# A fused attention + state-space gradient kernel: part of GpSimd's table work moved from the attention loop to the channel loop, and matmul bursts placed in other half-steps

## The chip, the cores and the metric

The kernel runs on one core of one Trainium2 chip. The metric is the device time of one execution in microseconds (us); lower is better. Before the change three runs gave 3099.37, 3094.06 and 3100.29 us, median 3099.37.

## What is computed

The reference is a forward pass and its gradients. For one sequence of S = 2048 tokens of width D = 576 it mixes two branches with a sigmoid gate and returns the output and twelve gradients for a given `grad_out` (bfloat16 in and out):

```
qkv = x @ wqkv;  a = softmax(q k^T / sqrt(18)) v @ wo            # 32 heads of width 18
P[d,n,l] = exp(dt[d] * A[d,n] * l),  l = 0..2047, N = 128 states  # complex
K[d,l]   = Re sum_n C[d,n] dt[d] B[d,n] P[d,n,l]
b = causal_convolution(u, K) + u * Dskip
out = g * a + (1 - g) * b,   g = sigmoid(sum(x * gate_w))
outputs: out, and d/d(x, wqkv, wo, A, B, C (re and im), log_dt, Dskip, gate_w)
```

What matters here: the convolution works in blocks of 128 positions and needs, for each channel d and state n, the table E[d] of complex powers z^l with z = exp(dt A), l = 0..127. It depends on the parameters alone, so it can be made at any time before its channel is worked on.

## The kernel before

**Stages.** One stage after the other: projections and parameters (to about 206 us of the profiled span), attention forward and backward (206 to 2302), the channel loop of the state-space branch (2302 to 2874), and the final products.

**Attention** (line 339 on) goes by units: 8 groups of 4 heads x 4 blocks of 512 queries = 32 units. A unit has 32 half-steps, and G counts them over all units. In half-step G TensorE makes two row-tiled matmuls of the forward pass (`P1`: tile ps_P<-QaT_g,KaT_g, line 709), and, for the unit that lies OFF = 39 half-steps behind, two matmuls of recomputed scores (`P3`: ps_P<-KaT_g,QaT_g) and two of the probability gradient (`P2`: ps_P<-dOaT,VaT_g). ScalarE makes exp of P1 (tile PT, line 802) and exp of P3 (tile eb, line 807); VectorE multiplies P2 by PT (tile ds, line 812, two a half-step). P1 and P3 share two PSUM buffers (tag S), P2 has two of its own (dP).

Besides, each half-step has one burst, by its phase `ph` = (G - 39) % 4, into one PSUM buffer (tag accB) that VectorE then empties:

| ph | burst | filler matmuls ahead of it (NFILL) | emptied by VectorE |
|---|---|---|---|
| 0 | accV, 8 matmuls | 0 | dvacc, line 508 |
| 1 | accQ, 8 matmuls | 0 | dqa, line 528 |
| 2 | accK, 16 matmuls | 1 | dkacc, line 556 |
| 3 | dst_p, 4 transposes of ds; in one half-step of a unit instead the transposes of the forward result (accF, line 411) | 3 | dsT, line 464; or rl, Ob |

A filler multiplies one constant by another (J_bf by ident_bf, tile accF or accK) and its result is overwritten. The forward sum accO<-PT,Vtok_g (4 matmuls for every second half-step's worth of PT, line 741) is issued in the half-steps of phase 0 and 1, after P2. The order on TensorE is by hand: P1(G), burst of G - 1, P3(G), P2(G), accO if it is due. At the end of a unit's forward pass the accO sum is copied (oT, line 407), transposed (f1), divided by its row sums (rl, Ob, lines 416 and 419), GpSimd makes dOa and prod (lines 421 and 423), and VectorE's dl (line 429) needs prod (f2).

**GpSimd in attention.** It makes all of E: 36 groups of CE = 16 channels, each of 78 instructions. 30 of them are small (powers of z, tiles eT and eG); then come 8 pairs of channels of 6 instructions each (two products et<-eG,eT and one sum Eo<-et,et, 128x256, for the real and again for the imaginary part, line 571), and after every second pair a DMA writes 4 channels to DRAM (E_d<-Eo, line 619). The instructions stand in a list with estimated costs; `e_emit(G)` issues the share due at half-step G, between G = 10 and 994, and nothing in the first three half-steps of a unit. GpSimd also packs gradients (dtk, line 446, and the DMA dqkv_d, line 447) and issues the DMAs put_x and put_gy (lines 663 and 667).

**Channel loop** (line 1136): 18 blocks of 32 channels, iteration i = -1 to 17. VectorE runs the scan of block i: 14 dependent steps of three instructions (tz line 997, tz line 1000, HG line 1001), then wa and wb (1016), Rw (1022, 1023), and the products pq (1067, 1095). ScalarE casts hR and gR (1008) between scan and pq, and in every second iteration prepares RX (891 to 893) ahead of these. TensorE turns E (etp, 958), and makes uvp, yp and the sums of pq. E comes back from DRAM in halves of a block (1 MB each, tile E1n, line 967, six buffers). GpSimd only makes two small sums an iteration, SS<-m, lines 1103 and 1104. The order on the compute engines is that of the code; DMA issues on SP are placed by the scheduler.

Of the kernel before, what the change touches and what calls it, by code (L numbers as in the profile page):

```python
# [20 lines left out]
def build(tc, aps, dbg_aps=None, stages=("s1", "attn", "post", "s4", "final")):  # L21
# [40 lines left out]
    with ExitStack() as gctx:  # L62
# [274 lines left out]
        go_v = go2.rearrange("(t p) d -> p t d", p=P)  # L337
        x_v = x2.rearrange("(t p) d -> p t d", p=P)
        if "attn" in stages:
            KB = 512  # L340
            NQ = S // KB
            TPQ = KB // P
            DA = HP
            NFILL = (0, 0, 1, 3)
            with ExitStack() as ctx:
# [212 lines left out]

                CE = 16
                EH = 4  # L560
                NA, NBT = P // 16, 16
                T_ = work.tile([P, 2, CE, NBT + 1], F32, tag="eT", bufs=1, name="eT")
                G_ = work.tile([P, 2, CE, NA], F32, tag="eG", bufs=1, name="eG")
                for t_ in (T_, G_):
                    nc.gpsimd.memset(t_[:, 0, :, 0], 1.0)
                    nc.gpsimd.memset(t_[:, 1, :, 0], 0.0)
                eops = []
                ez = {}

                def pl(out, a, b, op):  # L570
                    nc.gpsimd.tensor_tensor(out, a, b, op=op)  # L571

                def e_tmp(k):
                    return work.tile([P, 2 * P], F32, tag=f"et{k}", bufs=1, name=f"et{k}")

                def load_z(k):
                    ez[k] = work.tile([P, 2, CE], F32, tag="ez", bufs=2, name="ez")
                    nc.gpsimd.dma_start(ez[k], par_d[:, 12:14, k * CE:(k + 1) * CE])

                def emit_power(dst, src, lo, n, sq):  # L580

                    x = src[:, :, :, 1:1 + n]
                    st = []

                    def mul(ri):
                        w_ = e_tmp(ri)[:, 0:2 * CE * n].rearrange("p (r c m) -> p r c m", r=2, c=CE)
                        pl(w_, x, sq[:, ri].unsqueeze(1).unsqueeze(3).to_broadcast([P, 2, CE, n]), A.mult)
                        st.append(w_)
                    est = 0.21 + 2 * CE * n * 0.0018
                    eops.append((est, lambda: mul(0)))  # L590
                    eops.append((est, lambda: mul(1)))
                    est = 0.2 + CE * n * 0.002
                    eops.append((est, lambda: pl(dst[:, 0, :, lo:lo + n], st[0][:, 0], st[1][:, 1], A.subtract)))
                    eops.append((est, lambda: pl(dst[:, 1, :, lo:lo + n], st[0][:, 1], st[1][:, 0], A.add)))

                Eo = {}

                def e_main(k, c):
                    q = k * CE + c
                    for ri in range(2):  # L600
                        st = []

                        def mul(gi, ti, st):
                            if ti == gi == 0 and q % EH == 0:
                                Eo[q // EH] = work.tile([P, EH, 2, P], BF, tag="Eo", bufs=2, name="Eo")
                            w_ = e_tmp(gi)
                            pl(w_.rearrange("p (c a b) -> p c a b", c=2, b=NBT),
                               G_[:, gi, c:c + 2, :].unsqueeze(3).to_broadcast([P, 2, NA, NBT]),
                               T_[:, ti, c:c + 2, 0:NBT].unsqueeze(2).to_broadcast([P, 2, NA, NBT]), A.mult)
                            st.append(w_.rearrange("p (c l) -> p c l", c=2))  # L610

                        def add(ri, st):
                            o_ = Eo[q // EH][:, q % EH:q % EH + 2, ri, :]
                            if ri == 0:
                                pl(o_, st[1], st[0], A.subtract)
                            else:
                                pl(o_, st[0], st[1], A.add)
                                if (q + 2) % EH == 0:
                                    nc.gpsimd.dma_start(E_d[:, q + 2 - EH:q + 2], Eo.pop(q // EH))
                        eops.append((0.64, lambda mul=mul, ri=ri, st=st: mul(0, ri, st)))  # L620
                        eops.append((0.64, lambda mul=mul, ri=ri, st=st: mul(1, 1 - ri, st)))
                        eops.append((0.74 + 1.0 * (ri == 1 and (q + 2) % EH == 0), lambda add=add, ri=ri, st=st: add(ri, st)))

                for k in range(D // CE):
                    eops.append((0.25, lambda k=k: nc.gpsimd.tensor_copy(T_[:, :, :, 1], ez.pop(k))))
                    for n in (1, 2, 4, 8):
                        emit_power(T_, T_, n + 1, n, T_[:, :, :, n])
                    eops.append((0.25, lambda: nc.gpsimd.tensor_copy(G_[:, :, :, 1], T_[:, :, :, NBT])))
                    for n, m in ((1, 1), (2, 2), (4, 3)):
                        emit_power(G_, G_, n + 1, m, G_[:, :, :, n])  # L630
                    if k + 2 < D // CE:
                        eops.append((0.0, lambda k=k: load_z(k + 2)))
                    for c in range(0, CE, 2):
                        e_main(k, c)
                e_total = sum(x[0] for x in eops)
# [17 lines left out]
                for g0, nm, g, m in sorted(lds):  # L653
                    if g0 < 0:
                        load_piece(nm, g, m)
                    else:
                        at(("pre", g0), lambda nm=nm, g=g, m=m: load_piece(nm, g, m))
                for k in range(2):
                    at(("pre", 4), lambda k=k: load_z(k))
                NTOT = NU * NST  # L660
# [22 lines left out]
                for G in range(NTOT + OFF + 24):  # L683
# [48 lines left out]
                    tail = []  # L732
                    if G % 4 in (3, 0) and G >= 3:
                        i_ = (G - 3) // 4 * 2 + (1 if G % 4 == 0 else 0)
                        u_, i_ = divmod(i_, NT)
                        if u_ < NU:
                            g, b = units[u_]
                            if i_ == 0:
                                accO[(g, b)] = apsp.tile([P, KB], F32, tag="accO", name="accO")
                            for j in range(4):  # L740
                                mm(accO[(g, b)][HP * j:HP * (j + 1), :], lhsT=grp_t[g]["Vtok", i_ // TPQ][:, i_ % TPQ, HS * j:HS * j + HP], rhs=UN[(g, b)]["PT"][i_][:, j, :],
                                   start=(i_ == 0), stop=(i_ == NT - 1), tile_position=(0, HP * j))
                            if i_ == NT - 1:
                                f0, f1, f2 = post_forward(g, b, accO.pop((g, b)))
                                tail.append(f0)
                                at(("f1", G + 2), f1)
                                at(("f2", G + 4), f2)

                    def late(G=G, G2=G2, ph=ph):

                        evs = []
                        if ph in (0, 1, 2):
                            ACC.append(accB(("accV", "accQ", "accK")[ph]))
                            fill(ACC[0], NFILL[ph])
                        elif 0 <= G2 < NTOT or ("f1", G) in todo:
                            acc_f = accB("accF")
                            fill(acc_f, NFILL[3])
                            for f in todo.pop(("f1", G), []):
                                evs.append(f(acc_f))
# [68 lines left out]
                assert not todo and not packs, (todo.keys(), packs)  # L828
                assert e_done[1] == len(eops) and not Eo
        if "s4" in stages:  # L830
# [11 lines left out]
            with ExitStack() as ctx:  # L842
# [122 lines left out]
                def load_en(b, h):  # L965
                    dG = b * CB + h * GS
                    En = blk(b)["En"][h] = pw.tile([P, GS, 2, P], BF, tag="E1n", bufs=6, name="E1n")
                    nc.sync.dma_start(En, E_d[:, dG:dG + GS])
# [137 lines left out]
                def t0_load(b):  # L1106
# [5 lines left out]
                    nc.sync.dma_start(T0w.rearrange("p j c -> p (j c)"), src)  # L1112

                m_load(0)
                load_rx(0)
# [16 lines left out]
                load_en(2, 0)  # L1132
                load_en(2, 1)
                m_part(1, 0)
                m_part(1, 1)
                for i in range(-1, NBLK):
# [28 lines left out]
                    if cur:  # L1165
                        if nx:
                            t0_load(i + 1)
                        ybp(i, 0)
                        ybp(i, 1)
                        pairs1(i)  # L1170
                    if cur and mb is not None:
                        load_en(mb, 0)
                        load_en(mb, 1)
                    if sb is not None:
                        turn_e(sb, 0, 0, 4)
                        m_sum(sb)
                        m_fin(sb)
                    if cur:
                        pairs2(i)
# [262 lines left out]
```

## Time and profile before

| what | value |
|---|---|
| median of three runs | 3099.37 us |
| the profiled execution's own time | 3094.2 us |
| its span, first to last instruction | 3092.5 us |
| busy: PE, DVE, ACT, POOL | 2608.6, 2464.7, 2395.3, 1799.7 us |
| mean granted TensorE clock | 0.921 |
| HBM read and written | 144.48 MB, 99.69 MB |

PE is TensorE's matmul (PEld its weight load), DVE VectorE, ACT ScalarE, POOL GpSimd, SP the engine that issues most DMAs. A group of instructions is named by line, engine, operation and out<-in tiles; "idle before" is the time for which its engine stood still just ahead of it. A DMA's line is that of its issue. Most TensorE instructions are recorded by a helper on line 30 and are told apart by tile.

### The profile page before, as it was taken

The page shows a single profiled execution, that of the slowest core. Times are in us where ns is not written, and L with a number is a line of the kernel's source. Part 1 is how long each engine was busy: PE and PEld are TensorE (multiplying, and loading weights), DVE is VectorE, ACT ScalarE, POOL GpSimd, SP SyncE. Part 2 cuts the span into 40 slices and gives each one's busy share as a digit, 9 for nine tenths or more (in the row PEclk, how much of TensorE's full clock was granted, in tenths as well). Part 3 has the DMA queues.
Part 4 walks back from the last instruction along what each step waited for, and adds up shares of the span by engine and source line. Part 5 has one row for each costly group of instructions (what it writes and reads, how often), then busy time and mean ns, then how long its engine had stood idle before and what let it go on. Part 6 is the DMA issues. An engine that isn't in the chain of part 4 may idle for free. (4 is left out here: it accounts for less than half of the span.)

```text
span 3092.5 us, 70491 instructions
## 1 busy us (share of the span) xinstructions
PE 2608.6 (84%) x27147; PEld 1202.5 (39%) x27147; DVE 2464.7 (80%) x4531; ACT 2395.3 (77%) x2765; POOL 1799.7 (58%) x3371
## 2 busy tenths in 40 slices
PE   4768999899899899889889989989866887786679
PEld 2432232232233233223223323323225777776347
DVE  4436898898899899889889989989964888888634
ACT  2458999999899899999899989989836677675111
POOL 0038888988888889888898888988110000000010
PEclk8878999999999899999999999999987888888789
DMA  8757999899989999989998998898788887772885
GB/s 221 154 142 129 173 165 180 156 168 166 163 166 164 170 163 165 178 158 167 164 165 163 172 171 159 167 172 162 133 151 243 213 208 204 206 200 79 228 205 132
DMA packets 1409063, 529.41 MB, mean 171 GB/s; under 512 B 1303487, under 2 KB 1378849, under 8 KB 1399509
## 3 DMA queue, kind: packets, MB, share of 16 engines
q1 hardware_dynamic: 1380212, 464.27, 78.5%
q0 software_dynamic: 20624, 53.26, 6.6%
q10 hardware_dynamic: 7888, 7.38, 0.8%
q8 instruction: 212, 3.47, 0.4%
q14 instruction: 127, 1.03, 0.1%
HBM read 144.48 MB, written 99.69 MB: 79 GB/s over the span
## 5 line engine op out<-in xcount | busy, mean ns | idle before, releaser
L812 DVE TENSOR_TENSOR ds<-ps_P,PT 128x512 bf16<-128x512 f32 x2048 | 1312.3, 681 | 18.5 <-PE ps_P L30 14.4
L807 ACT ACTIVATE eb<-ps_P 128x1024 bf16<-128x1024 f32 x1024 | 1058.1, 1033 | 125.1 <-PE ps_P L30 120.7
L802 ACT ACTIVATE PT<-ps_P 128x1024 bf16<-128x1024 f32 x1024 | 1058.7, 1037 | 41.1 <-PE ps_P L30 39.1
L571 POOL TENSOR_TENSOR et<-eG,eT 128x256 f32<-128x256 f32 x1152 | 700.1, 629 | 35.5
L30 PE MATMUL ps_P<-dOaT,VaT_g 32*128 32x512 bf16 x2048 | 561.9, 390 | 51.3 <-DVE ds L812 43.8
L30 PE MATMUL ps_P<-QaT_g,KaT_g 32*128 32x512 bf16 x2048 | 413.6, 398 | 124.7 <-ACT PT L802 110.0
L571 POOL TENSOR_TENSOR Eo<-et,et 128x256 bf16<-128x256 f32 x576 | 418.7, 727 | 42.4
L30 PE MATMUL ps_P<-KaT_g,QaT_g 32*128 32x512 bf16 x2048 | 406.2, 389 | 1.4 <-ACT eb L807 1.0
L1103 POOL TENSOR_TENSOR SS<-m 128x96 f32<-128x96 f32 x18 | 7.8, 431 | 556.9 <-ACT m L1101 556.9
L30 PEld LDWEIGHTS <-KaT_g 32*128 32x128 bf16 x2048 | 135.4, 92 | 432.7 <-issue 430.9
L30 PEld LDWEIGHTS <-QaT_g 32*128 32x128 bf16 x2048 | 114.9, 91 | 310.4 <-issue 288.3
L30 PE MATMUL accF<-ident_bf,J_bf 128*128 128x512 bf16 x783 | 225.8, 399 | 10.0 <-DVE gb L556 10.0
L30 PE MATMUL accO<-PT,Vtok_g 128*32 128x512 bf16 x2048 | 213.2, 403 | 0.0
L464 DVE COPY dsT<-dst_p 128x512 bf16<-128x512 bf16 x224 | 95.0, 424 | 111.0 <-PE dst_p L463 109.9
L30 PEld LDWEIGHTS <-J_bf 128*128 128x128 bf16 x1103 | 89.1, 100 | 226.3 <-issue 194.6
L30 PE MATMUL accK<-dsT,Qtok_g 128*32 128x256 bf16 x4096 | 166.0, 284 | 0.0
L30 PE MATMUL accQ<-ds,Ktok_g 128*32 128x512 bf16 x2048 | 158.9, 387 | 2.8 <-DVE gb L508 1.5
L30 PE MATMUL accV<-eb,dOa 128*32 128x512 bf16 x2048 | 159.0, 388 | 2.2 <-DVE dsT L464 1.6
L959 ACT COPY E1e<-etp 128x1024 bf16<-128x1024 bf16 x144 | 135.8, 1040 | 16.8 <-PE etp L958 16.8
L30 PE MATMUL yp<-Rw,E1n 128*128 128x30 bf16 x1152 | 67.7, 232 | 83.7 <-DVE Rw L1022 69.1
L30 PEld LDWEIGHTS <-E1n 128*128 128x128 bf16 x2304 | 96.7, 109 | 101.2 <-issue 100.7
L508 DVE TENSOR_TENSOR dvacc<-dvacc,accV 128x512 f32<-128x512 f32 x192 | 130.1, 678 | 0.1
(243 smaller groups left out, 3911.6 us busy)
## 6 DMA issues: line engine op xcount, KB each, us to landing
E_d<-Eo POOLq DMA_DIRECT2D x144, 256.0 KB, 3.9
E1n<-E_d SPq DMA_DIRECT2D x36, 1024.0 KB
xs<-xb_d SPq DMA_DIRECT2D x18, 1024.0 KB
T0w<-Kp_d SPq DMA_DIRECT2D x18, 1024.0 KB
Md_d<-mst SPq DMA_DIRECT2D x36, 288.0 KB
dsT<-ds SPq DMA_TRANSPOSE x512
dqkv_d<-dtk POOLq DMA_DIRECT2D x96, 72.0 KB, 4.4
QKV_d<-stg SPq DMA_DIRECT2D x12, 504.0 KB
```

The lines of the kernel that those rows point to most:

```text
L30: return nc.tensor.matmul(out, lhsT=lhsT, rhs=rhs, start=start, stop=stop, **kw)
L464: return lambda: nc.vector.tensor_copy(U["dsT", p][:, 1, 0:TPQ, :], pt_)
L508: nc.vector.tensor_tensor(o_, a_, acc, op=A.add)
L571: nc.gpsimd.tensor_tensor(out, a, b, op=op)
L802: nc.scalar.activation(U["PT"][i][:, j:j + 2, :], ps, ACT.Exp)
L807: nc.scalar.activation(e, ps, ACT.Exp)
L812: nc.vector.tensor_tensor(U["ds"][i][:, j, :], ps, U["PT"][i][:, j, :], op=A.mult)
L959: nc.scalar.copy(E_[:, 4 * q:4 * q + 4], pt_)
L1103: nc.gpsimd.tensor_tensor(o_[:, :, 0], m4[:, :, 0], m4[:, :, 3], op=A.subtract)
```

## The change

1. The last four of the 18 channel blocks, that is the last 8 of 36 groups of E, are no longer made in attention. The code of the list becomes a function `basis_ops(pool, k0, k1)`, used for groups 0 to 27 in attention and for groups 28 to 35 in the channel loop. There `basis_share(i)` issues a fifteenth of the 624 instructions in each of the iterations -1 to 13, ahead of `pairs2` and `sums` of that iteration.
2. Forward sums move from phases 0 and 1 to phases 3 and 2 (`G % 4` 3, 0 becomes 2, 1); f1 follows the last one at one half-step instead of two, f2 at three instead of four.
3. Fillers: NFILL goes from (0, 0, 1, 3) to (1, 0, 0, 2), and to none where f1's transposes come.
4. E1n has five buffers instead of six, and the second half of block i + 2 is loaded in iteration i between the two ybp, not with its first half one iteration earlier.

```diff
-            NFILL = (0, 0, 1, 3)
+            NFILL = (1, 0, 0, 2)
...
-                for k in range(D // CE):
+            for k in range(k0, k1):
...
+                eops, load_z01 = basis_ops(work, 0, KE)
...
-                    if G % 4 in (3, 0) and G >= 3:
-                        i_ = (G - 3) // 4 * 2 + (1 if G % 4 == 0 else 0)
+                    if G % 4 in (2, 1) and G >= 2:
+                        i_ = G // 4 * 2 - (1 if G % 4 == 1 else 0)
...
-                                at(("f1", G + 2), f1)
-                                at(("f2", G + 4), f2)
+                                at(("f1", G + 1), f1)
+                                at(("f2", G + 3), f2)
...
-                            fill(acc_f, NFILL[3])
+                            fill(acc_f, 0 if ("f1", G) in todo else NFILL[3])
...
-                    En = blk(b)["En"][h] = pw.tile([P, GS, 2, P], BF, tag="E1n", bufs=6, name="E1n")
+                    En = blk(b)["En"][h] = pw.tile([P, GS, 2, P], BF, tag="E1n", bufs=5, name="E1n")
...
+                eops4, load_z4 = basis_ops(pw, KE, D // CE)
+                load_z4()
+
+                def basis_share(i):
+                    want = len(eops4) * min(1.0, (i + 2) / (NBLK - 3))
+                    while e4[0] < want:
+                        eops4[e4[0]][1]()
+                        e4[0] += 1
...
-                load_en(2, 1)
...
                         ybp(i, 0)
+                        if sb is not None:
+                            load_en(sb, 1)
                         ybp(i, 1)
                         pairs1(i)
                     if cur and mb is not None:
                         load_en(mb, 0)
-                        load_en(mb, 1)
                     if sb is not None:
                         turn_e(sb, 0, 0, 4)
                         m_sum(sb)
                         m_fin(sb)
+                    basis_share(i)
                     if cur:
                         pairs2(i)
                         sums(i)
```

## The prediction, made before the changed kernel was run

> **What bounds the kernel now.** I read the busy time by stage first, then the waits, then the order of time inside one cycle of each loop. In the table by stage the columns are the stretch in us, its length, then busy us (and instructions) of PE, PEld, DVE, ACT, POOL, the TensorE clock, the DMA share and GB/s. The two rows are the full attention stretch and the channel loop:
>
> ```profile
> 366.00:2221.00 1855.00, 1683.61 (x16712) 556.24 (x16710) 1644.42 (x2901) 1735.36 (x1857) 1605.34 (x2987) 0.97 0.94 165
> 2351.00:2874.00 523.00, 399.84 (x6648) 378.81 (x6646) 454.91 (x936) 353.31 (x520) 15.00 (x34) 0.82 0.70 181
> ```
>
> Attention has four engines at 87 to 94% and the DMAs at 0.94. The channel loop has VectorE at 87% and GpSimd empty. The list of waits (us in total, times, longest) names what the first stage loses:
>
> ```profile
> ACT eb L807 <- PE ps_P L30: 120.7, 271, 4.4
> DVE dsT L464 <- PE dst_p L463: 109.9, 216, 1.2
> DVE dl L429 <- POOL prod L423: 32.3, 13, 4.2
> ```
>
> In a steady cycle of four half-steps, from the timelines of PE and ACT (start, duration):
>
> ```profile
> 1617.06 0.39 PE L30 MATMUL ps_P<-QaT_g,KaT_g 32*128 32x512 bf16 x2 [0.24 <-ACT PT L802]
> 1617.38 0.82 PE L30 MATMUL accF<-ident_bf,J_bf 128*128 128x512 bf16 x3
> 1618.26 0.38 PE L463 MATMUL dst_p<-ident_bf,ds 128*128 128x128 bf16 x4
> 1618.57 0.39 PE L30 MATMUL ps_P<-KaT_g,QaT_g 32*128 32x512 bf16 x2
> ```
> ```profile
> 1615.93 1.07 ACT L802 ACTIVATE PT<-ps_P 128x1024 bf16<-128x1024 f32 x1
> 1619.06 1.02 ACT L807 ACTIVATE eb<-ps_P 128x1024 bf16<-128x1024 f32 x1 [0.21 <-PE ps_P L30]
> ```
>
> P1 starts 1.13 us after the start of the PT that frees its buffer, takes 0.32, then comes the burst (0.88 of fillers, 0.31 of transposes), then P3, and the eb 0.49 after P3. So this eb comes 1.13 + 0.32 + 0.49 = 1.94 plus the burst after that PT. ScalarE alone would start it three exps later; exps follow each other at 0.907, so 2.72. A burst of up to 0.78 is free; phase 3 has 1.19, 0.41 too much. Eight exps are 7.26, and 7.26 + 0.41 = 7.67: the steady cycle measures 7.66.
>
> The third wait is GpSimd's lag, here in its and DVE's timeline:
>
> ```profile
> 1269.89 1.24 POOL L667 DMA_DIRECT2D gyb_d<-gyr_d  x1
> 1271.15 0.69 POOL L421 TENSOR_TENSOR dOa<-dO_b,rl 128x288 bf16<-128x288 bf16 x1
> 1272.63 0.45 DVE L429 TENSOR_REDUCE dl<-prod 128x16 f32<-128x288 f32 x1 [4.01 <-POOL prod L423]
> ```
>
> rl was there at 1266.4; dOa stood behind table work, packs and a DMA issue. Such a cycle lasts 13.1 instead of 7.7. From the PT at 366.5 to the one at 2219.2 there are 927 half-steps: 64.0 us a unit, where undisturbed units take 61.4.
>
> **What the Trainium skill says.** Three places.
>
> "SBUF — State Buffer", section "Who interferes with whom": a VectorE instruction with two SBUF inputs contends with a GpSimd instruction that reads SBUF, and whichever comes second waits for the other. The trace agrees. In attention VectorE reads PSUM in its large operations (ds is 681 ns with GpSimd busy or not). In the channel loop nearly all it does has two SBUF inputs, and the only two GpSimd instructions there already cost it time:
>
> ```profile
> 2450.73 0.40 POOL L1103 TENSOR_TENSOR SS<-m 128x96 f32<-128x96 f32 x1 [28.66 <-ACT m L1101]
> 2450.74 0.54 DVE L1000 TENSOR_TENSOR tz<-tz,UV 128x128 f32<-128x128 f32 x1
> 2451.09 0.45 POOL L1104 TENSOR_TENSOR SS<-m 128x96 f32<-128x96 f32 x1
> 2451.31 0.38 DVE L1001 TENSOR_TENSOR HG<-tz 128x128 f32<-128x128 f32 x1
> ```
>
> Both VectorE operations take 0.29 elsewhere. A bound for the table's own size comes from attention's one small SBUF-only operation, median 0.20:
>
> ```profile
> 1915.87 1.22 POOL L571 TENSOR_TENSOR et<-eG,eT 128x256 f32<-128x256 f32 x2
> 1916.06 0.53 DVE L430 TENSOR_SCALAR dOa<-dl 128x16 bf16<-128x16 f32 x1
> ```
>
> "TensorE: Matmul & The Clock Gate", "Part 1": TensorE falls to half clock after a window of little activity, which is why fillers matter. In the stretch 2245 to 2265 PE is busy 83% and the clock is 1.00, so one filler less should do no harm.
>
> "DMA: Bandwidth & Descriptors", "Issuing engines are not separate DMA queues": all issues share the 16 DMA engines. The trace agrees as far as the DMA share of 0.94 sums all queues.
>
> **The change, part by part.**
>
> *Bursts and fillers.* New bursts: phase 3, two fillers 0.59 + 0.31 = 0.90 (0.12 over); phase 0, one filler 0.32 + accV 0.59 = 0.91 (0.13 over); phases 2 and 1, 0.56 each, under. The two excesses follow each other and don't add, since the second counts from a PT that the first hasn't delayed. Cycle: 7.26 + 0.13 = 7.39. The moved accO (0.33) goes into the 0.24 to 0.29 for which P1 of phases 2 and 3 now waits for PT; if that cover is gone it costs up to 0.1 a cycle. What is late next is VectorE: its idle time per cycle falls from 0.74 (0.24 before dkacc, 0.50 before dsT) to some 0.4, which must take the unit's extra oT, rl, Ob, dl, about 1.6 us. I take 0.6 a unit (bounds 0.1 and 1.0). accO of the next unit now starts right behind oT's copy: within that 0.6. A unit: 8 x 7.39 + 0.6 = 59.7.
>
> *Less GpSimd work in attention.* The table is 1456 us (all rows of lines 571, 625, 628), spread over 984 half-steps: 47.3 a unit; E_d issues with their wait 4.2; a pack 1.53, nine in the units that finish a group of heads; dOa and prod 1.4; put_x, put_gy and table loads 2.3. A heavy unit asks for 69 us and has 61 to 67: it lags, and the following unit inherits it, which is where the 13 waits lie. With 28 of 36 groups it asks for 58, below 59.7. The stalls go; next is a pack waiting for gT, hidden unless dOa is behind it.
>
> *DMAs in attention.* The E_d writes shrink by 8/36, some 1.6% of the DMA time. At 59.7 against 64.0 the share of 0.94 would be 0.99. I let the seven heavy units take 4 us more (bounds 0 and 8).
>
> Attention: 29 x (64.0 - 59.7) = 125, minus 28, saves 97.
>
> *Table work in the channel loop.* 624 instructions in 15 shares of 41.6, 323 us of GpSimd time, which itself is covered (37 us an iteration). The two shares of i = -1 and 0 run in the start-up before the first scan, where VectorE is idle for 47.7 us: nothing. The other 13 start behind SS, 5 us into a scan, and meet VectorE without gaps. Its next operation waits until GpSimd's reads are over: 0.085 for a second 128x96 (HG 0.38 against 0.29). The release comes 0.25 after the start of a 128x96 (from 2450.73 and the 0.25 lost) and 0.51 after that of a 128x256 (0.19 + 0.32 lost). So a product costs 0.085 + 0.26 = 0.345, a sum, 0.10 longer, 0.445. A share has 8.5 triplets (1.135 each) and 15 small ones (about 0.06): 10.6, of which 0.3 falls in short gaps. Bounds: 0.085 whatever the size, 3.5 a share; and the whole 0.63, 26 a share. I take 10.3: 13 x 10.3 = 134. Even iterations have a cover of their own: pq waits about 4.0 for hR because ScalarE is at RX; a later scan end swallows this, 6 x 4.0 = 24. Cost 110. SS stands behind the share, but a share stretched to about 33 us still ends inside an iteration of some 38.
>
> *Loads of E1n.* One megabyte is issued later and a buffer is gone. It must land between the first yp and the next k0, about 12 us; at 181 GB/s it moves in 5.8. 8.4 MB of E_d writes are added at a share of 0.70. I take 3 us (0 to 20).
>
> Sum: 3094.2 - 97 + 110 + 3 = 3110. That run lies 5 us under the median of 3099.37; I forecast 3110 for the median as well.
>
> **The rivals.** About 0.2%, 6 us, is what a measurement of this kernel can tell from no change.
>
> A, the forecast: both effects, near balance; its own range is 3085 to 3135, with slower likelier.
>
> B, faster: the port costs VectorE little. Place: the scans of blocks 1 to 13. If each of the 541 contended instructions costs the 0.085 of an SS, it is 46 - 24 = 22, and the time 3094 - 97 + 22 + 3 = 3022; halfway, with full relief of the DMAs, some 3045. It decides below (97 - 3 + 24) / 541 = 0.22 per instruction; I have 0.248. For it: only two GpSimd instructions in a row were seen. Against: the 0.32 lost to a 128x256.
>
> C, DMA-bound attention: with the share near 0.99, dsT, gT and loads arrive late in all units, and attention saves only 50: 3157. For it: heavy units already have little idle DMA time. Against: quiet units run 61.4 at 0.93.
>
> D, the port or the clock costs more: GpSimd instructions cost their full length (13 x 26 - 24 = 314, time 3314), or the missing filler lets the clock fall (0.3 a matmul burst, over 100). The 0.51 release, and the clock of 1.00 at 83%, speak against.
>
> That the change doesn't do what it says can be excluded from the order of GpSimd's instructions: some 40 stand between each two SS.
>
> **How the numbers follow.** A 0.45 (of it 0.25 slower, 0.09 within 6 us, 0.11 faster), B 0.24, C 0.20, D 0.11. Faster 0.35, same 0.09, slower 0.56. The range leaves out D and the ends of B and C, 2 in 10: 3035 to 3170.
>
> **What would show it.** Right: cycles of 7.4 and units of 60 in attention; dl's wait on prod near nothing; P3 of phase 0 and 1 the late ones; in the channel loop L997 to L1001 at 0.6 to 0.8 instead of 0.29 to 0.43, iterations of about 37 us instead of 27 and 31, and pq no longer waiting for hR. Wrong: those rows unchanged while GpSimd is busy (B); dkacc or ds waiting for dsT's DMA (C); PEclk below 0.9 in attention, or DVE idle between scan steps (D).

## The result and the profile after

The changed kernel takes 3183.15 us (median of 4 runs, 3179.93 to 3185.61) against 3097.36 us for the kernel before (4 runs): a ratio of 1.0277, 95% interval 1.0259 to 1.0294. The forecast was 3110, with a range up to 3170. The profiled execution took 3179.93 us, with a span of 3178.2; before it was 3094.2 and 3092.5. So 85.7 us of span are to be found.

All times of cycles and units below are differences of start times of the PT exps, taken from the trace: a cycle is four half-steps, a unit eight cycles. Units are counted from 0 by the P1 side; the "heavy" ones are the second of each group of four (5, 9, ... 29), in which the gradients of the group before are stored and packed, the "following" ones come right behind, the other 14 of units 3 to 30 are "quiet".

| stretch | before | after | change | forecast |
|---|---|---|---|---|
| first PT to last PT (attention) | 2012.6 | 1974.9 | -38 | -97 |
| last PT to first scan | 131.8 | 129.3 | -2 | 0 |
| first scan to last scan (channel loop) | 496.1 | 621.6 | +126 | +113 |
| last scan to the end | 245.4 | 244.6 | -1 | 0 |

The loop is 13 us over its forecast; attention gave 59 us less than it should. Within attention, mean us of a unit:

| units | before | after | forecast |
|---|---|---|---|
| quiet (14) | 61.6 | 61.8 | 59.7 |
| heavy (7) | 68.3 | 67.1 | 63.7 |
| following (7) | 64.8 | 61.3 | 59.7 |

Only the following units were clearly relieved. The table by stage, in the columns of the one in the prediction, for the full attention stretch and the channel loop after:

```profile
358.00:2184.00 1826.00, 1695.50 (x16413) 534.28 (x16412) 1640.11 (x2901) 1733.86 (x1857) 1286.10 (x2369) 0.96 0.93 164
2312.00:2961.00 649.00, 399.78 (x6653) 379.61 (x6651) 617.64 (x936) 356.31 (x520) 461.08 (x632) 0.75 0.59 160
```

GpSimd's 1605 us in attention became 1286, and yet the others hardly got fuller for it: PE is busy 93% of the stretch (before 91), VectorE 90 (89), ScalarE 95 (94), and the DMA share is 0.93 (0.94). In the loop the same 936 VectorE instructions take 617.6 us instead of 454.9. The list of waits of the kernel after (us in total, times, longest):

```profile
POOL dOa L504 <- DVE rl L499: 398.7, 32, 40.2
...
DVE dsT L547 <- PE dst_p L546: 130.6, 211, 1.5
...
ACT hR L1015 <- DVE HG L1008: 81.7, 15, 12.4
...
PEld L30 <- DMA dOaT<-dOa: 22.6, 8, 4.8
...
PE ps_P L30 <- DMA dOaT<-dOa: 20.7, 8, 4.3
```

The wait of dl for prod, 32.3 us before, is gone: GpSimd is now ready ahead of rl in all 32 units and waits 398.7 us for it. In its place stand eight waits of PE for the transposed dOaT, up to 4.3 us each; two are in units 1 and 2, the other six in six of the seven heavy units. In the loop, pq no longer waits for hR; hR waits for VectorE.

How a heavy unit goes after the change, unit 5, which starts at 480.0 and whose second cycle lasts 14.15 us. VectorE (start, duration):

```profile
488.53 0.45 DVE L512 TENSOR_REDUCE dl<-prod 128x16 f32<-128x288 f32 x1
489.01 0.30 DVE L513 TENSOR_SCALAR dOa<-dl 128x16 bf16<-128x16 f32 x1
```

SP's queue:

```profile
487.79 2.18 SPq L827 DMA_TRANSPOSE dsT<-ds  x1
490.02 1.52 SPq L468 DMA_TRANSPOSE Ktok_g<-QKV_d  x1
491.64 1.21 SPq L525 DMA_TRANSPOSE gT<-gb  x1
492.95 2.41 SPq L827 DMA_TRANSPOSE dsT<-ds  x1
495.45 0.98 SPq L514 DMA_DIRECT2D O_d<-Ob  x1
496.54 1.49 SPq L516 DMA_TRANSPOSE dOaT<-dOa  x1
```

PE:

```profile
500.78 0.61 PE L30 MATMUL ps_P<-dOaT,VaT_g 32*128 32x512 bf16 x2 [4.27 <-DMA dOaT<-dOa]
```

dOa is complete at 489.3. SP comes to its transpose only at 496.5, since it is still working off, one behind the other, what was queued ahead. In quiet and following units SP comes to it 9.3 to 10.5 us into the unit, in heavy ones 13.4 to 16.5. In the kernel before, the heavy units show 13.7 to 16.0, with dl at 9.5 to 12.9, where quiet units have 8.8: GpSimd's lag lay within a queue that was late in any case.

The channel loop after, groups of VectorE (count, busy us, mean ns, idle us before):

```profile
L1004 DVE TENSOR_TENSOR tz<-HG,par 128x256 f32<-128x256 f32 x252 | 151.0, 599 | 8.6
L1008 DVE TENSOR_TENSOR HG<-tz 128x128 f32<-128x128 f32 x252 | 120.0, 476 | 8.6
L1007 DVE TENSOR_TENSOR tz<-tz,UV 128x128 f32<-128x128 f32 x252 | 112.1, 445 | 8.7
```

Before, the three took 430, 298 and 295 ns on average over the same loop. Iterations last 33 to 44 us while a share of the table runs, and 27 to 29 behind the last share.

### The profile page after: what moved, and what is told of

The parts are those of the page before. It is cut to its first block, busy times and chain, and to the rows that moved or that the text cites. A ratio compares the mean times of both kernels' runs of the same rounds, so it can differ in the third digit from the quotient of the medians.

```text
span 3178.2 us, 69914 instructions
## 1 busy us (share of the span) xinstructions
PE 2615.8 (82%) x26822; PEld 1179.1 (37%) x26822; DVE 2622.7 (83%) x4531; ACT 2397.2 (75%) x2765; POOL 1934.3 (61%) x3375
## 5 line engine op out<-in xcount | busy, mean ns | idle before, releaser
L356 POOL TENSOR_TENSOR et<-eG,eT 128x256 f32<-128x256 f32 x1152 | 755.6, 677 | 35.5
L30 PE MATMUL ps_P<-dOaT,VaT_g 32*128 32x512 bf16 x2048 | 605.5, 390 | 41.3 <-DMA dOaT<-dOa 20.7
L356 POOL TENSOR_TENSOR Eo<-et,et 128x256 bf16<-128x256 f32 x576 | 435.9, 757 | 42.7
L30 PEld LDWEIGHTS <-KaT_g 32*128 32x128 bf16 x2048 | 142.0, 92 | 379.9 <-issue 366.4
L504 POOL TENSOR_TENSOR dOa<-dO_b,rl 128x288 bf16<-128x288 bf16 x32 | 21.5, 671 | 398.7 <-DVE rl L499 398.7
L30 PEld LDWEIGHTS <-Vtok_g 128*32 128x32 bf16 x2048 | 56.5, 93 | 274.7 <-issue 274.0
L1004 DVE TENSOR_TENSOR tz<-HG,par 128x256 f32<-128x256 f32 x252 | 151.0, 599 | 8.6
L30 PE MATMUL accF<-ident_bf,J_bf 128*128 128x512 bf16 x458 | 146.9, 404 | 11.4 <-DVE gb L639 11.3
```

Of the source, the lines that this page charges most:

```text
L30: return nc.tensor.matmul(out, lhsT=lhsT, rhs=rhs, start=start, stop=stop, **kw)
L1004: nc.vector.tensor_tensor(tz, HG[:, :, k - 1, :].unsqueeze(1).to_broadcast([P, 2, 4, CB]), ZZ, op=A.mult)
```

## The experiments

Each kernel ran on the chip beside the kernel before. Ratios are to the kernel before, with a 95% interval.

**The two halves of the change, each alone.**

The split of the table without the new bursts:

```diff
-            NFILL = (1, 0, 0, 2)
+            NFILL = (0, 0, 1, 3)
...
-                    if G % 4 in (2, 1) and G >= 2:
+                    if G % 4 in (3, 0) and G >= 3:
...
-                            fill(acc_f, 0 if ("f1", G) in todo else NFILL[3])
+                            fill(acc_f, NFILL[3])
```

> The changed kernel with the old bursts, old fillers and old place of the forward sums; only the table is split. Theory 1 (heavy attention units are held by SP's queue, not by GpSimd; only the units after them are relieved): heavy units stay near 67 us with dOaT issued 12 to 16 us into the unit, the six units behind them fall from 66 to 61.4, the channel loop stays near 649: 3097 - 29 + 126 = 3194 us. Rival (the shorter cycle of the new bursts crowds the DMAs, GpSimd's relief would have worked without it): heavy units fall to 62 as well, some 3160.

Measured 3192.36 us, ratio 1.0314 (1.0294 to 1.0333). Quiet units 61.5, following 61.6 (from 64.8), heavy 68.3 as before, although prod is on time in every one, with dOaT still reached 13.4 to 14.7 us into the unit. From first scan to last 619.3. Theory 1 holds: relief of GpSimd helps the following units only, also where no shorter cycle crowds the DMAs.

The new bursts without the split, on the kernel before:

```diff
-            NFILL = (0, 0, 1, 3)
+            NFILL = (1, 0, 0, 2)
...
-                    if G % 4 in (3, 0) and G >= 3:
+                    if G % 4 in (2, 1) and G >= 2:
...
-                            fill(acc_f, NFILL[3])
+                            fill(acc_f, 0 if ("f1", G) in todo else NFILL[3])
```

> The kernel before with only the new bursts, fillers and place of the forward sums; the whole table stays in attention, the channel loop is the old one. Theory 1 (a cycle now ends on VectorE's round trip to PE at 7.47, and most units lose 1.1 us to a half clock): quiet units 60.6 to 61.6, lagging units about as before, loop 523: 3097 - 10 = 3087 us, at best 3080. Rival (the bursts alone are worth the forecast 1.7 us a unit): 3060. Rival (with shorter units GpSimd lags more, and the gain is eaten up or worse): 3100 to 3120.

Measured 3087.21 us, ratio 0.9963 (0.9949 to 0.9976). Quiet units 61.4, following 65.4, heavy 68.1. The bursts are worth 0.4%, where the forecast gave them 1.7 us of each of 29 units.

**The channel loop: GpSimd's reads.**

```diff
             def pl(out, a, b, op):
-                nc.gpsimd.tensor_tensor(out, a, b, op=op)
+                if blank:
+                    nc.gpsimd.memset(out, 0.0)
+                else:
+                    nc.gpsimd.tensor_tensor(out, a, b, op=op)
...
-                eops4, load_z4 = basis_ops(pw, KE, D // CE)
+                eops4, load_z4 = basis_ops(pw, KE, D // CE, True)
```

> The changed kernel with every table product and sum of the channel loop replaced by a memset of the same output; the tables of the last four blocks are zeros, their writes to memory and the loads of E1n are the same. Theory (GpSimd's reads of SBUF hold VectorE's two-input operations): tz, HG and wa/wb back at 0.43, 0.30 and 2.15 us, loop near 523 to 530, 3183 - 120 = 3063 us. Rival (any GpSimd access of SBUF contends, writes too): half or more of the 126 stays, above 3110. Rival (E1n's later load and one buffer less, or the added writes, are what costs): above 3150 with VectorE's rows short and yp or k0 waiting.

Measured 3056.59 us, ratio 0.9878 (0.9853 to 0.9903). First scan to last 492.8, against 496.1 before and 621.6 after. The groups of VectorE in the loop of this run:

```profile
L1007 DVE TENSOR_TENSOR tz<-HG,par 128x256 f32<-128x256 f32 x252 | 108.4, 430 | 8.6
L1011 DVE TENSOR_TENSOR HG<-tz 128x128 f32<-128x128 f32 x252 | 75.1, 298 | 8.6
L1010 DVE TENSOR_TENSOR tz<-tz,UV 128x128 f32<-128x128 f32 x252 | 74.3, 295 | 8.7
```

and of GpSimd:

```profile
L357 POOL MEMSET et<- 128x256 f32 x238 | 68.7, 323 | 0.0
```

VectorE is back to the nanosecond, although GpSimd writes the same tiles beside it and the same rows of E_d go to memory. So the whole 126 us go with the instructions that read; the writes, the later load of E1n and its missing buffer cost nothing that shows. That agrees with the section "Who interferes with whom" of the Trainium skill's page "SBUF — State Buffer", by which a VectorE instruction with two SBUF inputs contends with a GpSimd instruction that reads SBUF, not with one that only writes it. One limit: the memsets also take half as long as the instructions that they replace.

**Heavy units: who makes dOaT late.**

In the next run dOaT's transpose was given to ScalarE's queue:

```diff
+                        if b != 1 or g == 0:
+                            f3(nc.sync)
+
+                    def f3(eng):
                         U["dOaT"] = work.tile([P, TPQ, P], BF, tag="dOaT", name="dOaT")
-                        nc.sync.dma_start_transpose(out=U["dOaT"], in_=U["dOa"].rearrange("p t a b -> p (t a b)"))
+                        eng.dma_start_transpose(out=U["dOaT"], in_=U["dOa"].rearrange("p t a b -> p (t a b)"))
+                    if b == 1 and g > 0:
+                        at(("f3", now[0] + 4), lambda: f3(nc.scalar))
```

> The changed kernel, but in the second unit of each group (the heavy ones) the transpose that makes dOaT is issued by ScalarE, one half-step later in its program, and no longer stands in SP's queue. Theory 1 (in heavy units dOaT waits for SP to work off what was queued ahead of it): P2 no longer waits for dOaT, heavy units fall from 67 to some 62.5, 7 of them: 3183 - 32 = 3151 us; ScalarE pays about 1.2 us in each. Rival (the 16 DMA engines are full there, so dOaT lands late from any queue, or dsT is late in its place): above 3170.

Measured 3213.65 us, ratio 1.0390 (1.0352 to 1.0428). Neither theory was tested, for two reasons. The edit sat one unit too late: the dOaT that a heavy unit waits for belongs to the first unit of the group, whose forward sum ends in the second one; with b equal to 1 the edit reached the following units. Heavy units stayed at 68.2, following ones rose from 61.3 to 67.2. And the second queue is no way round. ScalarE in such a unit:

```profile
565.51 1.29 ACTq L520 DMA_TRANSPOSE dOaT<-dOa  x1
566.90 1.02 ACT L815 ACTIVATE PT<-ps_P 128x1024 bf16<-128x1024 f32 x1 [5.81 <-issue]
```

dOa was ready at 559.3; ScalarE stood on a semaphore for most of the 5.81 us (the longest such wait ahead of this line is 6.26 us) and then issued. The Trainium skill's page "DMA: Bandwidth & Descriptors", section "Silent corruption: two transposing streams in flight at once", says that the first transpose of a later stream must wait until the earlier stream's transposes are complete. All seven such waits of the run last 4.9 to 6.3 us, and in each SP issues a transpose of dsT; that fits, but no run takes it apart further.

The same question, asked within SP's queue: what stood ahead of dOaT is put behind it.

```diff
+                        nc.sync.dma_start_transpose(out=U["dOaT"], in_=U["dOa"].rearrange("p t a b -> p (t a b)"))
                         nc.sync.dma_start(O_d[:, b * TPQ:(b + 1) * TPQ, 4 * g * DH:4 * (g + 1) * DH], Ob.rearrange("p t a b -> p t (a b)"))
-                        nc.sync.dma_start_transpose(out=U["dOaT"], in_=U["dOa"].rearrange("p t a b -> p (t a b)"))
...
-                                (g0 + OFF + 8 * m - 13, "Ktok", g, m)
+                                (g0 + OFF + 8 * m - 9, "Ktok", g, m)
...
+                def store_at(n):
+                    return "pre", n + 5 - n % NST if n % NST < 5 else n
```

> The changed kernel with a lighter SP queue ahead of the transpose that makes dOaT: O_d behind it, dO_b and Ktok loaded 8 and 4 half-steps later, gradient stores that would fall just ahead of it put just behind it (one gb buffer more). Theory 1 (in heavy units dOaT waits in SP's queue): SP reaches it at 9.5 to 11 us of the unit instead of 12 to 16.5, heavy units fall from 67 to some 63: 3183 - 28 = 3155 us. Rival (the 16 DMA engines are full in these units whatever the order): heavy units stay at 66 or more, above 3172.

Measured 3150.63 us, ratio 1.0166 (1.0146 to 1.0186), some 34 us less than the changed kernel (the difference of the two ratios, times 3097; so below). Heavy units 62.8 instead of 67.1. Unit 5 of this run, VectorE:

```profile
496.01 0.30 DVE L513 TENSOR_SCALAR dOa<-dl 128x16 bf16<-128x16 f32 x1
```

SP's queue:

```profile
496.78 1.51 SPq L515 DMA_TRANSPOSE dOaT<-dOa  x1
```

Half a microsecond now lies between dOa and its transpose, where it was 7.2. The DMA engines were not full while the transpose stood in the queue: their share over those 7.2 us of the changed kernel (489.3 to 496.5) is 0.87, against 1.04 over as long a stretch from dOa on in this run (496.3 to 503.5; a packet counts where it starts, so that a share can pass 1). So it was the order of the queue and not full engines that held the heavy units. What each part of the edit gives, the later loads, the later stores and the added gb buffer, was not separated.

**Quiet units: the half clock and the fillers.**

In 13 of the 21 quiet and following units of the changed kernel, PE falls to half speed for a few us, from 11 to 13 us into the unit on; before, no quiet unit shows it. PE in unit 7 of the kernel after:

```profile
620.84 1.04 PE L30 MATMUL accK<-dsT,Qtok_g 128*32 128x256 bf16 x16
621.81 0.60 PE L30 MATMUL ps_P<-KaT_g,QaT_g 32*128 32x512 bf16 x2
```

The same rows take 0.62 and 0.39 a cycle later. My first guess was the fillers that the change drops in the half-step of oT's transposes:

```diff
-                            fill(acc_f, 0 if ("f1", G) in todo else NFILL[3])
+                            fill(acc_f, NFILL[3])
```

> The changed kernel with the two fillers kept in the half-step that transposes oT. Theory 1 (their absence lets TensorE fall to half clock for 3.4 us behind it, 1.1 us in 17 of 28 units): no half-clock stretch in quiet units, cycle 1 at 8.3 everywhere, 3183 - 18 = 3165 us. Rival (the fillers cost what they save: 0.61 a unit on PE's way to P3): 3175 to 3190.

Measured 3189.87 us, ratio 1.0289 (1.0257 to 1.0321), no gain. The first cycle grows from 7.35 to 7.75 us, and the half clock still comes in 8 of the 21 units. The run without GpSimd's reads, whose attention code is that of the changed kernel, shows it in 8 as well, so the count differs between executions of the same code. This guess falls; the rival is right.

The drop begins one cycle behind these transposes, in the accQ and accK bursts, so fillers go there:

```diff
-                            fill(ACC[0], NFILL[ph])
+                            fill(ACC[0], NFILL[ph] + (ph > 0 and G % NST in (4, 5)))
```

> The changed kernel with one filler more in each of two half-steps of every unit, the accQ and accK bursts of the second cycle, where VectorE works off oT, rl, Ob and dl and PE waits for ds. Theory 1 (the half clock there is set off by PE's idle time just before): no half-clock stretch in quiet units, cycle 1 at 8.3 to 8.6 everywhere: 3183 - 12 = 3171 us. Rival (the fillers lie on PE's way to the next P3, or the half clock comes all the same): 3183 to 3200.

Measured 3163.53 us, ratio 1.0227 (1.0189 to 1.0266), some 15 us less than the changed kernel, though the two intervals still overlap a little. PE at the same place in unit 7 of this run:

```profile
618.89 0.62 PE L30 MATMUL accK<-dsT,Qtok_g 128*32 128x256 bf16 x16
```

Quiet units are 60.7 (from 61.8), and of the 21 only one still shows a half clock. Heavy units are at 68.3 (from 67.1), which takes back half of what the others gain in the trace. What sets the half clock off is not settled: in the 3.8 us ahead of it PE was busy for 3.46 us in unit 7, more than in unit 4 (3.37) and in the kernel before (3.29), which kept full clock. Only that two matmuls more in this place keep it away is shown: one of 21 units here and none in the next run, against 8 or 13 without them.

Both repairs together, the fillers and the lighter queue:

> The changed kernel with the lighter SP queue ahead of dOaT and the two fillers of the second cycle together. If the queue (-33) and the half clock (-20) are separate losses: 3183 - 53 = 3130 us, attention some 90 us shorter than before, near the 97 of the forecast. If they are one loss seen twice: 3150.

Measured 3137.71 us, ratio 1.0142 (1.0120 to 1.0164): 42 us less than the changed kernel, where the two alone gave 34 and 15. The gain over the lighter queue alone is some 7 us, within the intervals, and in the profiled executions attention lasts 1946.1 us from first PT to last with both and 1946.0 with the queue alone. Quiet units are shorter (60.7 against 61.2) and heavy ones longer (65.0 against 62.8): in them VectorE waits for the DMA of dsT nine times, 9.8 us in all, where it was three times and 1.8 us. Why is not shown, and so it stays open whether the two gains add up.

**Can the table stay in attention?** Since the loop cannot take it, seven runs tried to keep it in attention without the stalls. The first two give the heavy units less of it, and the last group of 36 to the prologue, ahead of the first scan:

```diff
-        KE = D // CE - 4 * (CB // CE)
+        KE = D // CE - 1
...
-                    want = len(eops4) * min(1.0, (i + 2) / (NBLK - 3))
+                    want = len(eops4)
...
+                e_w = [0.0 if G < 10 else 0.7 if G // NST % 4 == 1 and G >= 2 * NST else 1.0 for G in range(NU * NST - 30)]
```

> New bursts; 35 of the 36 table groups in attention, emitted at 0.7 of the rate in the heavy units and faster elsewhere; the last group in the prologue of the channel loop, none in the loop; dOaT of the heavy units from ScalarE's queue. Theory 1 (GpSimd's peak and SP's queue are what stalls attention, and VectorE in the loop must not be touched): all units 60.5 to 63, loop 526: 3087 - 60 = some 3025 us. Rival (on average GpSimd and the DMAs are too full to give the heavy units' share to others): units of 62 to 65 all over, 3065 to 3090.

> The same as the run with 35 groups in attention and the dOaT of heavy units on ScalarE's queue, but with the old bursts, fillers and place of the forward sums. Theory 1: units of 61.5, heavy ones 62 to 63: 3097 - 13 stalls x 5 = some 3035 us, a little above the one with new bursts. Rival (as there): 3070 to 3095.

Measured 3118.13 (1.0077, 1.0049 to 1.0106) and 3136.76 (1.0139, 1.0106 to 1.0172). Both carry the misplaced transpose of the ScalarE run, which costs some 6 us in each of 7 following units (67.1 with the new bursts), so they don't decide between their theories. They do show two things. With no share beside the scans the loop is back at 492.9 from scan to scan (new bursts). And a lower rate that begins with the heavy unit comes too late: prod ends 12.3 to 16.9 us into the heavy units there, later than with the even rate (9.0 to 14.3 with the new bursts, 9.5 to 12.9 with the old). The units ahead were given more.

A pause in the emission around the half-step in which rl comes, alone on the kernel before and together with the new bursts, the fillers and the lighter queue:

```diff
-                    if G % NST not in (0, 1, 2) or G >= NTOT:
+                    if 2 < G % NST < 27 or G >= NTOT:
```

> The kernel before with nothing but the pause in the emission of table work. Theory 1 (GpSimd's lag costs only because table work stands ahead of dOa; heavy units are held by SP's queue): units behind the heavy ones fall from 66 to 61.5, heavy ones stay near 67: 3097 - 25 = 3070 us. Rival (the lag only moves): 3090 to 3100.

> New bursts with the whole table in attention and the old channel loop, plus one filler in the accQ and accK bursts of the second cycle, plus a pause in the emission of table work from half-step 27 of a unit to half-step 2 of the next, so that GpSimd's queue is empty when rl comes. Theory 1: prod is on time in all units, the units behind the heavy ones fall from 66 to 61, no half clock in quiet units: 3087 - 20 - 30 = some 3040 us. Rival (GpSimd is asked for 97% of the time on average, so the lag only moves): 3065 to 3085.

> The run with the pause and the fillers, with the lighter SP queue ahead of dOaT as well. Theory 1: heavy units at 63 too: 3040 - 28 = some 3012 us. Rival (DMA engines full): as without it, 3040.

Measured 3106.07 (1.0023, 1.0012 to 1.0035), 3092.47 (0.9971, 0.9963 to 0.9978) and 3111.62 (1.0044, 1.0031 to 1.0057). No theory 1 holds. The lag moves, as the rival of the first two says, though both times lie some us above its range; the third is over 70 us slower than its own rival. Following units fall to 62.4, 60.9 and 60.6, but heavy units rise to 72.2, 73.4 and 76.5. The list of waits of the second of the three shows where the lag went:

```profile
DVE dl L429 <- POOL prod L423: 32.1, 12, 5.7
...
DVE ds L812 <- DMA dsT<-ds: 17.1, 10, 4.3
```

The wait for prod is as large as before the change, and there is a new one for dsT. In the seventh cycle of heavy unit 13 (start 1000.3) of that run, GpSimd and then SP's queue:

```profile
1047.12 0.42 POOL L446 COPY dtk<-gT 128x288 bf16<-128x288 bf16 x1
```

```profile
1047.57 1.19 SPq L442 DMA_TRANSPOSE gT<-gb  x1
1048.85 2.04 SPq L820 DMA_TRANSPOSE dsT<-ds  x1
```

SP had been at this gT since 1042.7; it goes on as soon as GpSimd's late pack has read one of the three gT buffers (1047.54), and the dsT transposes behind it stand for the same 4.9 us. So GpSimd's lag reaches PE through SP's queue. This was read from the timelines and not tested alone.

Last, no pause, but a rate of 0.8 over the 48 half-steps of each group in which gradients are packed, with the new bursts, the two fillers and the lighter queue; once with 35 groups in attention and one in the prologue, once with all 36:

```diff
+                e_w = [0.0 if G < 10 else 0.8 if 16 <= G % (4 * NST) < 2 * NST and G >= 4 * NST else 1.0 for G in range(NU * NST - 30)]
...
-                    want = e_total * min(1.0, max(0.0, (G - 10) / (NTOT - 40)))
+                    want = e_total * min(1.0, e_rate[G])
```

> New bursts, the two fillers and the lighter SP queue; 35 table groups in attention at 0.8 of the rate in the 48 half-steps of each group in which the gradients are packed, the last group in the prologue of the channel loop, none beside its scans. Theory 1 (GpSimd and SP have room if no unit is asked for more than it has): units of 60.6 to 62, loop some 526: 3097 - 75 = 3022 us. Rival (GpSimd at 96% has no room: packs late, gT held, SP's queue stuck behind it): 3060 to 3100.

> The same with all 36 groups in attention and the old channel loop. Theory 1: 3025 to 3035 us; rival: 3070 to 3110, as GpSimd is asked for 98%.

Measured 3053.11 us (0.9863, 0.9844 to 0.9882) and 3089.11 (0.9976, 0.9967 to 0.9985). The first is the best version of the study, 1.4% under the kernel before and 4% under the changed one, though 31 us over what I expected. Its units: heavy 65.2, following 60.6, quiet 62.9, up to 68.1. One wait of its list says in part why it isn't better:

```profile
DVE dl L512 <- POOL prod L506: 21.0, 13, 4.0
```

Thirteen units still find GpSimd behind. With one group more, 1/36 of the table, 36 us come back, 32 of them in attention (2013.2 us from first PT to last, against 1981.3), and dl waits for prod 21 times, 49.3 us in all. This points to GpSimd's average load: the last few per cent of it are the dear ones. The queue and the DMAs carry the added group too, and no run separates them from it.

## Why the prediction was wrong

The sum of the forecast was -97 + 110 + 3; measured are -38 (attention), +126 (loop) and -2 (the rest). The step that failed most is "The stalls go": with GpSimd on time, the heavy units were held by SP's queue. By the forecast's own steps:

- **Table work in the channel loop: right in mechanism, a little small.** VectorE's busy time in the loop grew by 617.6 - 454.9 = 162.7 us. The trace has 562 table instructions behind the start of the first scan, not 541, since the second share is not done when that scan starts. That is 0.29 us each; I had taken 0.248 (134 us), for the larger ones from a row of VectorE with only one input (dOa<-dl), a stand-in for the two-input case. Of the 162.7 us the wait of pq for hR gives back 38, where I had 24. Net 126 against 110. The bound of 0.085 each, on which rival B stood, is excluded. (A share has 16 small instructions, not 15, which changes nothing.)
- **Loads of E1n: 3 us forecast, none measured.** The run without reads keeps the late load and the missing buffer and is no slower in the loop than the kernel before.
- **Less GpSimd work in attention: "The stalls go" failed.** The wait on prod went as stated, and what was to be late next was named wrongly: not a pack, but SP's queue ahead of dOaT. I had the rows in hand. In the kernel before, SP issues dOaT in heavy units 13.7 to 16.0 us into the unit, as here in unit 17, which starts at 1259.7:

```profile
1269.66 2.40 SPq L820 DMA_TRANSPOSE dsT<-ds  x1
1272.16 1.04 SPq L431 DMA_DIRECT2D O_d<-Ob  x1
1273.39 1.19 SPq L433 DMA_TRANSPOSE dOaT<-dOa  x1
```

  An earlier dl doesn't move the rows ahead of it, and in the run with the split alone, with dl on time, SP came to dOaT at 13.4 to 14.7. Seven heavy units at 67.1 instead of 63.7 are 24 us; the run with the lighter queue, at 62.8, shows that this was the cause. The 4 us that I allowed the heavy units under "DMAs in attention" had the right place and the wrong mechanism, since not full engines (a DMA share of 0.87 during the wait in unit 5) but one queue's order was the limit.
- **Bursts and fillers: 7.39 forecast, 7.45 and 7.51 in turns measured.** This is 8 x 0.09 = 0.7 us a unit, 15 over the 22 units that are not heavy (the heavy ones have it within their 24). The steady cycle after, VectorE:

```profile
645.50 1.28 DVE L819 TENSOR_TENSOR ds<-ps_P,PT 128x512 bf16<-128x512 f32 x2
647.34 0.42 DVE L547 COPY dsT<-dst_p 128x512 bf16<-128x512 bf16 x1 [0.56 <-PE dst_p L546]
```

and PE:

```profile
646.25 0.61 PE L30 MATMUL accF<-ident_bf,J_bf 128*128 128x512 bf16 x2
646.92 0.38 PE L546 MATMUL dst_p<-ident_bf,ds 128*128 128x128 bf16 x4
```

  The transposes of ds start 0.67 after the two fillers, not the 0.59 that I took from a third less of three: they wait for the ds pair that VectorE ends at 646.78. So the third filler gave back only 0.21 of its 0.29, the burst is 0.98 instead of 0.90, and the forecast's own sum becomes 7.26 + 0.20 = 7.46. VectorE in turn does nothing until the transposes are done, 0.56 us. With its 6.87 to 6.91 us of busy time this fills its cycle too. The idle time that I left VectorE (some 0.4) can't all be used; what lies in a round trip is no reserve.
- **"One filler less should do no harm": failed.** The place that I looked at, PE at 83% and full clock, was another stretch, and the busy share is no guide here: in unit 7 PE was busy for 91% of the 3.8 us ahead of the half clock. In the second cycle of 13 of 21 units the clock halved, some 1.1 us a unit; with fillers there the quiet and following units are 16 us shorter in the trace, all 21 together. Rival D had named this cause, at over 100 us.
- **The unit's extra VectorE work: right.** I had 0.6 us a unit; without a half clock a unit lasts 60.5, which is 0.7 over eight cycles.

Together 24 + 15 + 16 = 55 of the 68 us that are missing over units 3 to 31; the rest is not accounted for. Rival C has the nearest time, 3157, but not its mechanism: it expected dsT and gT late in all units from full DMAs, and in the trace after VectorE nowhere waits for the DMA of dsT. So its nearness is luck. The forecast's range was too narrow because I let a miss in attention and a miss in the loop stand as rivals to each other; both came, in the same direction.

## What to carry to other kernels

Before costing the removal of a wait, write down for each later step when its issuer comes to it, and compare: where an in-order queue reaches the step late in any case, removing the wait gives nothing. An engine with free time may be poor cover for moved work if both it and the loaded engine read SBUF, the latter with two inputs: here each moved instruction cost 0.29 us. Measure that price on pairs of the same kind before moving many. And take the idle time of an engine that sits between its own result and an answer from another engine as occupied.

## What the runs showed of the hardware

- A GpSimd tensor_tensor beside VectorE instructions with two SBUF inputs cost VectorE 0.29 us on average and became longer itself (860 ns instead of 629 for a 128x256 product of f32); memsets of the same tiles, which are half as long, cost VectorE nothing (430, 298 and 295 ns, as before).
- TensorE fell to half clock for a few us after a stretch in which it was 91% busy by the trace, and not after others at 87 and 89%; two matmuls of 128x512 more kept it at full clock in 20 of 21 units, then in all 21. The busy share alone does not tell the cases apart. Where GpSimd was late again, in the run with 35 groups in attention, they did not suffice: 7 of 21 units fell, each one with a wait for prod.
- ScalarE stood 4.9 to 6.3 us on a semaphore ahead of each of seven transposes by DMA that it issued, while SP's queue had one of its own; no run shows what the semaphore stood for.
- In an in-order queue, 7.2 us passed between the data and its transpose with a DMA share of 0.87; with other transfers put behind it, it was 0.5 us.
